# Attention scores from three fp32r products instead of one fp32 product, in a kernel of windowed attention and a gated convolution

## The chip, the cores and the metric

One core of a Trainium2 chip. The metric is the device time of one execution in microseconds. Before the change it was 666.89 us, the median of three runs (666.77 to 667.21).

The engines are called PE (TensorE's matmuls; PEld is its weight loads), DVE (VectorE), ACT (ScalarE), POOL (GpSimd) and SP (the queue that issues the DMAs).

## The reference

Eight batches, eight heads, 576 positions, heads of 64. Attention looks back over a window of 128 positions, with a bias that falls linearly with distance (a slope per head). Its output, 4608 tokens of 512 features, goes through a feed-forward part with a convolution over three neighbouring positions and a sigmoid gate. Everything is computed in fp32 accuracy.

```
scores = q @ k.T / sqrt(64) - slope[h] * |i - j|,  masked to 0 <= i - j < 128
attn   = softmax(scores);  x = attn @ v            # heads put side by side: (8, 576, 512)
h      = relu(x @ w_in)                            # 512 -> 1024
conv   = sum over k of conv_w[k] * h shifted by k-1, zero beyond a batch's ends
out    = (h * sigmoid(conv)) @ w_out               # 1024 -> 512
```

## The kernel before, in words

The 4608 tokens are 36 tiles of 128. A batch has 4.5 tiles, so tiles 0, 9, 18 and 27 begin a batch exactly, tiles 4, 13, 22 and 31 contain a boundary in their middle, and tiles 5, 14, 23 and 32 begin half a tile into a batch. A tile's queries see its own keys and those of the tile before; a batch's exact first tile needs only its own.

[...] The type fp32r holds a rounded fp32 number and is one instruction. The kernel writes a number as a high half (its fp32r rounding) and a low half (the rest), and takes three products: high by high, high by low, low by high. Before the change it did so for the up-projection (L424) and the down-projection (L501), while the scores (L287, L289), the product with the values (L377) and the transposes (L263, L347) were fp32.

Steps of a tile t, by the short names that the order uses; u is one of two groups of four heads:

- LD, LV: fetch q and k, and v (L255), by SP. Q: eight transposes of q and k on PE (L263) into two PSUM tiles. QO: ACT copies both to SBUF (L267), into one of three slots of `qkT_all` (t modulo 3).
- S: scores (L289, in exact first tiles L287). For each u there are two PSUM tiles, for the even and the odd heads; an even head lies in rows 0 to 63, an odd one in rows 64 to 127, and the two are issued in turn.
- MA: DVE merges the keys of the previous tile into the own ones under a mask (L305; at batch boundaries a second mask), then scales and adds the bias (L318). RM: row extreme (L322). X: exponentials on ACT (L327), two heads to a piece. N: DVE normalizes (L338 to L340). T: transposes on PE (L347). RL: ACT copies them out (L352). SEL: POOL cuts the window's two triangles (L358, L361).
- AV: product with the values on PE (L377). XH: ACT writes its high half into the ring `ring` (L388). XL: DVE writes the low half (L392). XF: every fourth tile, a small copy at the ring's end (L397).

Steps of the feed-forward part run over 18 chunks of 256 tokens, four steps s to a chunk, two blocks of 128 of the 1024 features to a step:

- UH: up-projection, 12 matmuls of 256 columns a block (L424). HH: relu on ACT (L437). Z: the middle tap on ACT (L443) into `zp`, of which there is one buffer, so that the next Z waits for the gate of the step before. CV: the outer taps on DVE (L456); a chunk with a batch boundary inside is cut, four pieces for two. TH: tanh on ACT (L464). GT: the gate on DVE (L469). GH: high half on ACT (L479). GL: low half on POOL (L484).
- D: down-projection, 12 matmuls of 512 columns (L501). OB: after a chunk's fourth step ACT copies the two sums out and SP stores them (L514, L516).

Weights come as 16 blocks and the taps as one small block, and they arrive as 64-bit floating-point numbers that the kernel turns into high and low halves itself: F fetch, CL and SG on POOL (L161, L171), RS on ACT (L166), SH and V on DVE (L175; L181 or L185, then L188), H the high half on ACT (L195), then P and W for the low half. For a block in LOW_POOL or LOW_DVE the low half is one subtraction on that engine (L214); otherwise PE forms it in PSUM with three instructions (L206, L207) and ACT copies it out (L216). A block in SIGNS has its sign prepared on POOL, and DVE then needs one operation (L181) where it otherwise needs two (L175, L185).

Five PSUM buffers with the tag `tr` are shared by transposes, scores, the product with the values, the up-projections and the weights' low halves. Each engine takes its instructions in the order in which the pieces stand in three written lists: OPENING (tiles 0 to 5, steps 0 to 5, all weights), PERIOD (once for each tile from 6 to 35, with two steps) and TAIL (what is left). A number in PERIOD is relative: S0 is this tile, Q1 the next, AV-1 the last.

Of the kernel before, what the change touches and what calls it, by code (L numbers as in the profile page):

```python
# [21 lines left out]
def tile_alibi_window_attention_conv_glu(  # L22
# [154 lines left out]
    def w_bits(b):  # L177
        st, g = wst.pop(b), wgs[b]
        lo, hi = st[..., 0], st[..., 1]
        if b in SIGNS:  # L180
            nc.vector.scalar_tensor_tensor(  # L181
# [40 lines left out]

    raws, vraw, pts, sms, es, pas, rls, avs = {}, {}, {}, {}, {}, {}, {}, {}
    ring = cpool.tile([P, 2, NCC, RING + 4], F32R, name="ring")
# [37 lines left out]
        pts[t, u] = ps  # L264

    def qkT_out(t, u):
        nc.scalar.copy(out=qkT_all[:, t % SLOTS, u], in_=pts.pop((t, u)))  # L267

    def window(t):
        first = (t * P) % S  # L270
        slot = t % SLOTS
        if slot:
            win, prev, cur = slice(slot - 1, slot + 1), 0, 1
        else:
            win, prev, cur = slice(0, SLOTS, SLOTS - 1), 1, 0
        return first, slot, win, prev, cur

    def scores(t, u):
        first, slot, win, prev, cur = window(t)

        pss = [pst.tile([P, NG, 2, P], F32, name=f"sc{t}_{u}_{a}", tag="tr") for a in range(2)]
        for g in range(NG):
            for a in range(2):
                rows = slice(a * D, (a + 1) * D)
                qt = qkT_all[rows, slot, u, 0, g, :]
                if first == 0:
                    nc.tensor.matmul(pss[a][:, g, cur], qt, qkT_all[rows, slot, u, 1, g, :], start=True, stop=True)  # L287
                else:
                    nc.tensor.matmul(pss[a][:, g], qt, qkT_all[rows, win, u, 1, g, :], start=True, stop=True)  # L289
        sms[t, u] = pss  # L290


    def merge(t, u, a):
# [8 lines left out]
        shp = [P, 2, P]

        def put(mask, data):
            nc.vector.copy_predicated(out=s_cur, mask=mask.unsqueeze(1).to_broadcast(shp), data=data)  # L305
# [12 lines left out]
        nc.vector.scalar_tensor_tensor(out=heads, in0=s_cur, scalar=-0.125, in1=b, op0=ALU.mult, op1=ALU.add)  # L318
# [208 lines left out]
    TILE = {
        "LD": load, "LV": loadv, "Q": qk, "QO": qk_out, "S": scores, "MA": merge, "RM": rowmax,  # L530
        "X": lambda t, u, h: exps(t, u, range(2 * h, 2 * h + 2)),
        "N": normal, "T": attnT, "RL": attn_out, "SEL": select, "AV": av, "XH": x_hi, "XL": x_lo, "XF": xfin,
    }
# [23 lines left out]
    OPENING = """
    LD0 F1 F3 F0 CL0 CL1 Q0 LD1 QO0 S0.0 RS0 RS1 S0.1 LV0 H4 MA0.1.1 SG0 F2 CL3 MA0.1.0 LD2 MA0.0.1 RM0.1
    MA0.0.0 Q1 F4 CL2 LV4 QO1 X0.1.1 V0 S1.0 F7 X0.1.0 MA1.0.1 SG1 RM0.0 MA1.0.0 S1.1 H0 MA1.1.1 F5 Q2 P0
    RS2 N0.1 LD3 LV1 QO2 LD4 V1 S2.0 T0.1 X0.0.1 X0.0.0 F8 H1 MA1.1.0 F13 N0.0 W0 P1 RM1.0 X1.0.0 F10 X1.0.1  # L560
    W1 MA2.0.1 SG2 Q3 F9 SH5 CL4 CL7 LV2 RS4 QO3 SH4 RS3 V2 N1.0 T0.0 RL0.0 CL5 H2 S2.1 T1.0 SG3 RM1.1 S3.0
    P2 MA2.1.0 RL0.1 X1.1.0 X1.1.1 MA2.1.1 Q4 LD5 RL1.0 V3 RM2.1 MA2.0.0 MA3.0.0 H3 RM2.0 F6 X2.1.1 W2
    X2.1.0 RS5 N1.1 SEL0.0 SEL0.1 AV0 LV3 X2.0.0 P3 XF1 V4 W3 X2.0.1 T1.1 LD6 QO4 RS7 SH8 SEL1.0 V5 P4 CL13
    CL8 S3.1 N2.0 SG7 MA3.0.1 T2.0 RL1.1 H5 N2.1 LD8 MA3.1.0 SEL1.1 AV1 MA3.1.1 T2.1 W4 XH0 P5 RS8 RM3.0
    RL2.0 XH1 RM3.1 X3.1.1 SEL2.0 RL2.1 CL10 V8 X3.1.0 F11 SH9 X3.0.1 F12 XL1 SEL2.1 F16 S4.0 CL6 AV2 CL9 W5
    RS6 XF0 SG6 H8 XL0 MA4.0.0 XH2 N3.1 Q5 V7 P8 X3.0.0 QO5 H7 W8 P7 N3.0 SH10 XL2 T3.1 W7 CL11 RS9 UH0.0
    RS11 UH0.1 RL3.1 LD7 V6 T3.0 MA4.0.1 H6 RS10 HH0.1 HH0.0 SG11 RL3.0 S4.1 RM4.0 V10 Z0.0 V9 CV0.0 Z0.1
    UH1.0 CV0.1 H10 HH1.0 TH0 V11 RS13 F15 H9 GT0 W6 XF2 LV5 W10 UH1.1 UH3.1 HH1.1 XF3 Z1.0 UH2.0 Z1.1 CL15
    MA4.1.1 CV1.1 CV1.0 GH0 MA4.1.0 SEL3.0 SEL3.1 UH2.1 TH1 X4.0.0 GT1 X4.0.1 UH3.0 HH3.0 RM4.1 N4.0 HH2.0
    P9 SH12 AV3 HH3.1 CL12 HH2.1 T4.0 X4.1.0 SG13 W9 V13 S5.1 X4.1.1 N4.1 RS12 T4.1 H13 Z2.1 XH3 GL0 F14  # L570
    S5.0 Z2.0 V12 RL4.0 MA5.1.0 RL4.1 SEL4.0 H11 SEL4.1 W13 H12 CV2.0 CV2.1 AV4 P11 CL16 MA5.0.1 D0 TH2 GH1
    Z3.1 GT2 Q6 XH4 MA5.1.1 CV3.1 XL4 Z3.0 W12 GH2 XL3 XF4 GL1 RS16 MA5.0.0 CL14 W11 CV3.0 RS15 UH4.1 RS14
    RM5.0 RM5.1 SG15 SG14 LV6 X5.1.1 X5.0.1 V15 V14 UH5.1 H15 UH5.0 UH4.0 D1 TH3 X5.0.0 GT3 SG16 N5.0 X5.1.0
    T5.0 V16 HH4 H14 QO6 H16 Z4.1 GL2 W14 RL5.0 GH3 W15 LV7 D2 N5.1 CV4.1 T5.1 HH5 GL3 Z4.0 SEL5.0 W16 CV4.0
    TH4 RL5.1 GT4 SEL5.1 Z5.1 GH4 GL4 CV5.1 Z5.0 CV5.0 TH5 D3 GT5 OB3
    """
# [50 lines left out]
```

## Time and profile before

| | us |
|---|---|
| median of three runs | 666.89 |
| the profiled execution's own time | 667.78 |
| its span in the trace | 665.5 |
| scores of tile 6 begin | 104.28 |
| scores of tile 35 begin | 602.87 |
| one plain period (tile 20) | 17.08 |

The profile shows one execution. [...] A row of a timeline has the start, the length, the engine, the line of the kernel, the operation, what it writes and reads, and how many instructions are merged in it; in square brackets stands idle time before it and who ended it. A row of a group has busy time and the mean length of one in ns behind the bar, then idle time before the group. A row of a stretch has for each engine the busy time, with the number of instructions in brackets, then the granted clock of PE as a share, the share of the DMA engines and GB/s.

### The profile page before, as it was taken

The page shows a single profiled execution, that of the slowest core. Times are in us where ns is not written, and L with a number is a line of the kernel's source. Part 1 is how long each engine was busy: PE and PEld are TensorE (multiplying, and loading weights), DVE is VectorE, ACT ScalarE, POOL GpSimd, SP SyncE. Part 2 cuts the span into 40 slices and gives each one's busy share as a digit, 9 for nine tenths or more (in the row PEclk, how much of TensorE's full clock was granted, in tenths as well). Part 3 has the DMA queues.
Part 4 walks back from the last instruction along what each step waited for, and adds up shares of the span by engine and source line. Part 5 has one row for each costly group of instructions (what it writes and reads, how often), then busy time and mean ns, then how long its engine had stood idle before and what let it go on. Part 6 is the DMA issues. An engine that isn't in the chain of part 4 may idle for free.

```text
span 665.5 us, 13256 instructions
## 1 busy us (share of the span) xinstructions
PE 634.5 (95%) x4860; PEld 547.8 (82%) x4860; DVE 516.4 (78%) x1177; ACT 434.3 (65%) x1202; POOL 214.3 (32%) x319
## 2 busy tenths in 40 slices
PE   4888799999999999999999999999999999999997
PEld 3467587887888788888888888988888888888995
DVE  5998997778777888787777788778778888788554
ACT  3876775665766676666666766666676656666553
POOL 2353544333233322233233222223222233333321
PEclk9989999999999999999999999999999999999999
DMA  9878003232323223131403140404040403000001
...
DMA packets 120099, 47.00 MB, mean 71 GB/s; under 512 B 113356, under 2 KB 113380, under 8 KB 120036
## 3 DMA queue, kind: packets, MB, share of 16 engines
...
q14 instruction: 25, 0.20, 0.1%
...
## 4 chain that ended last, share of the span: by engine, by line
PE 56%; DVE 28%; ACT 9%; issue 4%; DMA 1%; SPq 0%; POOL 0%; POOLq 0%; DVEq 0%; ACTq 0%
PE p L424 21%; PE o L501 19%; DVE zp L456 12%; PE sc L289 5%; PE av L377 5%; ACT zp L443 4%; DVE sc L305 3%; DVE z L469 3%; PE pa L347 3%; DVE e L318 3%; PE pt L263 3%; ACT e L327 2%; DMA rqk<-in_k_dram 1%; DVE ring L392 1%; ACT zp L464 1%
## 5 line engine op out<-in xcount | busy, mean ns | idle before, releaser
L424 PE MATMUL p<-ring,wi 128*128 128x256 f32 (+1 forms) x1728 | 221.3, 284 | 8.3 <-DVE ring L397 3.6
L424 PEld LDWEIGHTS p<-ring,wi 128*128 128x128 f32 x1728 | 211.9, 189 | 14.5 <-issue 4.2
L456 DVE SCALAR_TENSOR_TENSOR zp<-hh,cw,zp 128x256 f32<-128x256 f32 (+7 forms) x384 | 162.2, 422 | 76.0 <-ACT zp L443 65.3
L501 PE MATMUL o<-wo,gh 128*128 128x512 f32 x576 | 186.1, 404 | 0.6 <-ACT ob L514 0.6
L327 ACT ACTIVATE e<-e,st 128x128 f32<-128x128 f32 x288 | 112.4, 393 | 96.3 <-DVE st L322 96.3
L358 POOL TENSOR_SCALAR_AFFINE_SELECT rl<-rl 128x512 f32<-128x512 f32 x64 | 41.1, 642 | 280.9 <-ACT rl L352 280.9
L501 PEld LDWEIGHTS o<-wo,gh 128*128 128x128 f32 x576 | 103.1, 188 | 26.8 <-issue 5.2
L484 POOL TENSOR_TENSOR gl<-z,gh 128x512 fp32r<-128x512 f32 x71 | 91.2, 1284 | 86.7 <-ACT gh L479 74.6
L501 PE MATMUL o<-wo,gl 128*128 128x512 f32 x288 | 114.7, 398 | 0.4 <-POOL gl L484 0.2
L443 ACT ACTIVATE zp<-hh,cw 128x256 f32<-128x256 f32 x144 | 69.0, 479 | 24.0 <-DVE z L469 15.8
L469 DVE SCALAR_TENSOR_TENSOR z<-zp,hh 128x512 f32<-128x512 f32 (+1 forms) x73 | 49.8, 682 | 29.3 <-ACT zp L464 27.1
L464 ACT ACTIVATE zp<-zp 128x512 f32<-128x512 f32 (+1 forms) x73 | 42.3, 579 | 45.1 <-DVE zp L456 42.4
L289 PE MATMUL sc<-qkT_all 64*128 64x256 f32 x512 | 68.4, 396 | 1.9 <-ACT rl L352 1.3
L377 PEld LDWEIGHTS av<-rl,rv 128*64 128x64 f32 x1088 | 59.2, 138 | 12.4 <-issue 8.2
L377 PE MATMUL av<-rl,rv 128*64 128x128 f32 x1088 | 68.8, 278 | 0.3
L501 PEld LDWEIGHTS o<-wo,gl 128*128 128x128 f32 x288 | 54.1, 188 | 13.7 <-POOL gl L484 1.2
L318 DVE SCALAR_TENSOR_TENSOR e<-sc,bias 128x256 f32<-128x256 f32 x144 | 61.1, 424 | 5.0
L289 PEld LDWEIGHTS sc<-qkT_all 64*128 64x128 f32 x512 | 48.5, 189 | 14.3 <-issue 5.6
L361 POOL TENSOR_SCALAR_AFFINE_SELECT rl<-rl 128x512 f32<-128x512 f32 x72 | 46.6, 647 | 36.9 <-ACT rl L352 29.2
L305 DVE COPY_PREDICATED sc<-m_prev,sc 128x256 f32<-128x256 uint8 x128 | 53.7, 420 | 1.7 <-PE sc L289 1.7
L327 ACT ACTIVATION_READ_ACCUMULATOR e<-e,st 128x1 f32 x288 | 54.4, 189 | 0.0
L340 DVE TENSOR_TENSOR e<-e,st 128x512 f32<-128x512 f32 x72 | 50.4, 700 | 2.5
...
## 6 DMA issues: line engine op xcount, KB each, us to landing
...
```

The lines of the kernel that those rows point to most:

```text
L289: nc.tensor.matmul(pss[a][:, g], qt, qkT_all[rows, win, u, 1, g, :], start=True, stop=True)
L305: nc.vector.copy_predicated(out=s_cur, mask=mask.unsqueeze(1).to_broadcast(shp), data=data)
L318: nc.vector.scalar_tensor_tensor(out=heads, in0=s_cur, scalar=-0.125, in1=b, op0=ALU.mult, op1=ALU.add)
L327: nc.scalar.activation(out=e[:, j, :], in_=e[:, j, :], func=AF.Exp, bias=st[:, 0, j : j + 1], scale=-1.0, accum_out=st[:, 1, j : j + 1],)
L340: nc.vector.tensor_tensor(out=e, in0=e, in1=st[:, 2, :].unsqueeze(2).to_broadcast([P, HU, P]), op=ALU.mult)
L377: nc.tensor.matmul(ps[a * D : (a + 1) * D, u * NG + g], vraw[tt][:, u * HU + j], rl[:, side, j], start=n == 0, stop=n == len(sides) - 1,)
L424: nc.tensor.matmul(ps, a[:, cc, f * P : (f + 1) * P], ring[:, i, cc, cols], start=n == 0, stop=n == last)
L443: nc.scalar.activation(out=zps[s][:, ff, :], in_=hhs[s][:, ff, 1 : 1 + CW], func=AF.Copy, scale=cw[:, 1, f : f + 1])
L456: nc.vector.scalar_tensor_tensor(out=z[:, ff, a:cut], in0=hh[:, ff, a + kk : cut + kk], scalar=cw[:, kk, f : f + 1], in1=z[:, ff, a:cut], ...
L469: nc.vector.scalar_tensor_tensor(out=zgs[s][:, ff], in0=zps[s][:, ff], scalar=1.0, in1=hhs[s][:, ff, 1 : 1 + CW], op0=ALU.add, op1=ALU.mult,)
L484: nc.gpsimd.tensor_tensor(out=gl, in0=zgs.pop(s), in1=as32(gh), op=ALU.subtract)
L501: nc.tensor.matmul(oos[c][m], g[:, ff, ms], w[:, f, :], start=f == 0 and n == 0, stop=f == NFC - 1 and n == 2)
```

## The change

- From tile 9 on (`SPLIT = 9`), ACT's evacuation of the transposed queries and keys (QO) writes fp32r, which is the high half. A new step QL subtracts this on DVE from the PSUM tile and writes the low half to `qkT_low`. The scores become three fp32r products, each summed in PSUM. Tiles 0 to 8 keep the fp32 product. QL for tile t+1 stands in PERIOD of tile t.
- Transposed queries and keys have two slots in place of three. The fp32 tile and the fp32r tile share one buffer, which changes its type at tile 9.
- The PSUM tiles of the transposes are given back by QL from tile 9 on, by QO before.
- OPENING, PERIOD and TAIL are written anew.
- SIGNS grows by blocks 5, 8, 9, 10 and 12. LOW_POOL has one block (9) in place of four, LOW_DVE gets block 6 as well. Eleven blocks take PE's way to the low half instead of nine.

The core of the diff:

```
-    SIGNS = {0, 1, 2, 3, 6, 7, 11, 13, 14, 15, 16}
-    LOW_POOL = {6, 10, 12, 13}
-    LOW_DVE = {14, 15, 16}
+    SIGNS = {0, 1, 2, 3, 5, 6, 7, 8, 9, 10, 11, 12, 13, 14, 15, 16}
+    LOW_POOL = {9}
+    LOW_DVE = {6, 14, 15, 16}
...
-    SLOTS = 3
+    SLOTS = 2
+    SPLIT = 9
     NG = HU // 2
-    qkT_all = cpool.tile([P, SLOTS, 2, 2, NG, P], F32, name="qkT_all")
+    qkT_low = cpool.tile([P, SLOTS, 2, 2, NG, P], F32R, name="qkT_low")
+    qkTs = {}
+
+    def qkT_of(t):
+        kind = F32 if t < SPLIT else F32R
+        if kind not in qkTs:
+            qkTs[kind] = apool.tile([P, SLOTS, 2, 2, NG, P], kind, name=f"qkT{t}", tag="qkT", bufs=1)
+        return qkTs[kind]
...
     def qkT_out(t, u):
-        nc.scalar.copy(out=qkT_all[:, t % SLOTS, u], in_=pts.pop((t, u)))
+        nc.scalar.copy(out=qkT_of(t)[:, t % SLOTS, u], in_=pts.pop((t, u)) if t < SPLIT else pts[t, u])
+
+    def qkT_rest(t, u):
+        if t >= SPLIT:
+            nc.vector.tensor_tensor(
+                out=qkT_low[:, t % SLOTS, u], in0=pts.pop((t, u)), in1=as32(qkT_of(t)[:, t % SLOTS, u]), op=ALU.subtract
+            )
...
+        keys = win if first else slice(slot, slot + 1)
+        top = qkT_of(t)
+        passes = ((top, top),) if t < SPLIT else ((top, top), (top, qkT_low), (qkT_low, top))
         for g in range(NG):
...
+            for n, (tq, tk) in enumerate(passes):
+                for a in range(2):
+                    rows = slice(a * D, (a + 1) * D)
+                    to = pss[a][:, g] if first else pss[a][:, g, cur]
+                    of = tk[rows, keys, u, 1, g, :] if first else tk[rows, slot, u, 1, g, :]
+                    nc.tensor.matmul(
+                        to, tq[rows, slot, u, 0, g, :], of, start=n == 0, stop=n == len(passes) - 1
+                    )
```

PERIOD before:

```
S0.0 S0.1 AV-1 XH-1 MA0.1.0 MA0.0.0 XL-1 D-2 XF-1 MA0.0.1 UH0.1 GH-1 RM0.0 MA0.1.1 UH0.0 X0.0.1 X0.0.0
HH0 Z0.0 RM0.1 LD3 UH1.1 Z0.1 N0.0 Q1 UH1.0 CV0.0 X0.1.1 GL-1 LV2 QO1 CV0.1 X0.1.0 HH1 T0.0 D-1 TH0
RL0.0 N0.1 GT0 T0.1 Z1.1 Z1.0 SEL0.0 CV1.0 RL0.1 SEL0.1 GH0 OB-1 OB-2 GL0 CV1.1 TH1 GT1
```

PERIOD after:

```
S0.0 S0.1 AV-1 MA0.0.1 D-2 XH-1 LV2 XL-1 XF-1 MA0.0.0 RM0.0 X0.0.0 MA0.1.0 UH0.1 UH0.0 UH1.1 GH-1 X0.0.1
HH0 MA0.1.1 Z0.0 Z0.1 Q1 LD3 RM0.1 UH1.0 X0.1.0 GL-1 X0.1.1 N0.0 QO1 CV0.0 HH1 T0.0 D-1 CV0.1 N0.1 TH0
OB-2 RL0.0 Z1.1 GT0 SEL0.0 Z1.0 QL1 T0.1 RL0.1 SEL0.1 CV1.0 GH0 CV1.1 OB-1 TH1 GL0 GT1
```

OPENING before begins `LD0 F1 F3 F0 CL0 CL1 Q0 LD1 QO0 S0.0 RS0 RS1 S0.1 LV0`; after, it begins `LD0 Q0 F1 QO0 S0.0 CL1 RS1 S0.1 MA0.0.0 MA0.1.1 LD1 F2 SG1 Q1`. In TAIL the pieces are the same ones; D-1 stands later, behind the up-projections of the next steps.

More of the change, by code (lines that the diff above doesn't have):

```diff
@@ L271, in window @@
         slot = t % SLOTS
[L272 to L275, printed above, removed]
+        win, prev, cur = slice(0, SLOTS), 1 - slot, slot
         return first, slot, win, prev, cur
@@ L281, in scores @@
         pss = [pst.tile([P, NG, 2, P], F32, name=f"sc{t}_{u}_{a}", tag="tr") for a in range(2)]
+        keys = win if first else slice(slot, slot + 1)
+        top = qkT_of(t)
+        passes = ((top, top),) if t < SPLIT else ((top, top), (top, qkT_low), (qkT_low, top))
         for g in range(NG):
[L283 to L289, printed above, removed]
+            for n, (tq, tk) in enumerate(passes):
[6 more added lines that the diff above has]
+                    )
         sms[t, u] = pss
@@ L525, in qk_out, with qk_rest @@
             qkT_out(t, u)
+    def qk_rest(t):
+        for u in range(2):
+            qkT_rest(t, u)
     TILE = {
-        "LD": load, "LV": loadv, "Q": qk, "QO": qk_out, "S": scores, "MA": merge, "RM": rowmax,
+        "LD": load, "LV": loadv, "Q": qk, "QO": qk_out, "QL": qk_rest, "S": scores, "MA": merge, "RM": rowmax,
         "X": lambda t, u, h: exps(t, u, range(2 * h, 2 * h + 2)),
@@ L557, in tile_alibi_window_attention_conv_glu @@
     OPENING = """
[L558 to L572, printed above, removed]
@@ L573, in tile_alibi_window_attention_conv_glu @@
-    RM5.0 RM5.1 SG15 SG14 LV6 X5.1.1 X5.0.1 V15 V14 UH5.1 H15 UH5.0 UH4.0 D1 TH3 X5.0.0 GT3 SG16 N5.0 X5.1.0
-    T5.0 V16 HH4 H14 QO6 H16 Z4.1 GL2 W14 RL5.0 GH3 W15 LV7 D2 N5.1 CV4.1 T5.1 HH5 GL3 Z4.0 SEL5.0 W16 CV4.0
-    TH4 RL5.1 GT4 SEL5.1 Z5.1 GH4 GL4 CV5.1 Z5.0 CV5.0 TH5 D3 GT5 OB3
+    LD0 Q0 F1 QO0 S0.0 CL1 RS1 S0.1 MA0.0.0 MA0.1.1 LD1 F2 SG1 Q1 MA0.1.0 V1 QO1 S1.0 F0 MA0.0.1 MA1.0.1 LD2
+    CL2 CL0 RM0.0 S1.1 RS2 RS0 F7 H1 F3 X0.0.0 SG2 F5 X0.0.1 MA1.1.1 SG0 LV0 Q2 MA1.0.0 F4 P1 QO2 V0 F9
@@ new lines, in tile_alibi_window_attention_conv_glu @@
+    RM0.1 S2.1 F8 N0.0 LD3 W1 X0.1.1 V2 MA1.1.0 MA2.1.1 T0.0 X0.1.0 RL0.0 H0 SEL0.0 P0 RM1.1 H2 S2.0 W0 CL3
+    MA2.1.0 CL5 X1.1.1 CL4 RS3 P2 N0.1 RM2.1 RS5 LD4 F10 T0.1 MA2.0.1 LV3 W2 MA2.0.0 RL0.1 RM1.0 X1.1.0 F13
+    RM2.0 SH4 X2.1.0 N1.1 RS4 X2.0.1 LV2 X2.0.0 Q3 SG3 SG5 T1.1 QO3 H4 X2.1.1 V4 N2.0 T2.0 V5 CL7 S3.1 XF1
+    X1.0.0 SEL0.1 RL2.0 F6 S3.0 RL1.1 CL10 LV1 V3 X1.0.1 MA3.1.0 H5 P5 LD5 MA3.0.1 N1.0 Q4 H3 MA3.0.0 XF3
+    N2.1 CL8 F14 P3 T1.0 AV0 W5 RS7 SG7 V7 QO4 MA3.1.1 S4.0 MA4.0.1 RL1.0 RM3.0 W3 S4.1 F12 LD6 CL6 H7
@@ new lines, in tile_alibi_window_attention_conv_glu @@
+    SEL1.0 MA4.0.0 P7 P4 RS8 X3.0.1 F11 W7 XH0 T2.1 SEL1.1 RS10 X3.0.0 LV4 MA4.1.0 AV1 RL2.1 W4 SEL2.0 SG8
+    SEL2.1 V8 AV2 H8 XL0 RS6 RM4.0 XH1 Q5 N3.0 SG6 XH2 QO5 CL12 XF0 P8 CL9 CL13 V6 X4.0.1 XL1 XL2 W8 MA4.1.1
+    T3.0 H6 RM3.1 UH0.0 XF2 SG10 RM4.1 RS9 SG9 UH0.1 V10 HH0.0 X4.0.0 UH1.1 S5.1 F15 Z0.0 F16 H10 HH0.1
+    X4.1.1 W6 N4.0 RL3.0 RS13 UH2.0 V9 CV0.0 X4.1.0 X3.1.0 Z0.1 UH1.0 MA5.1.1 H9 CV0.1 SG13 CL14 V13 HH1.1
+    SEL3.0 P10 LV5 N4.1 CL16 HH2.0 X3.1.1 UH2.1 TH0 W9 W10 GT0 H13 P13 HH1.0 HH2.1 T4.0 RS12 RL4.0 MA5.1.0
@@ new lines, in tile_alibi_window_attention_conv_glu @@
+    Z1.0 GH0 Z1.1 W13 SG12 UH3.0 T4.1 RL4.1 CL11 RS11 N3.1 S5.0 CV1.1 MA5.0.0 LV6 CV1.0 UH3.1 T3.1 TH1 V12
+    RL3.1 H12 GT1 SEL4.0 SEL4.1 SEL3.1 HH3.1 Z2.1 AV4 RS16 GL0 CL15 P12 Z2.0 MA5.0.1 RM5.1 SG11 XH4 AV3 D0
+    X5.1.0 CV2.0 XL4 HH3.0 CV2.1 SG16 XH3 V11 W12 X5.1.1 GH1 XF4 Q6 TH2 H11 QO6 LD8 RS15 GT2 P11 XL3 N5.1
+    GL1 RM5.0 UH5.1 SG15 W11 Z3.1 X5.0.0 V16 UH5.0 RS14 UH4.1 CV3.1 T5.1 SG14 HH5 V15 Z3.0 UH4.0 V14 H16
+    X5.0.1 GH2 RL5.1 H15 H14 CV3.0 LD7 GL2 TH3 HH4 D1 N5.0 GT3 Z4.1 W14 W15 CV4.1 D2 W16 GH3 GL3 T5.0 D3
@@ L576, in tile_alibi_window_attention_conv_glu @@
+    Z4.0 RL5.0 SEL5.1 CV4.0 LV7 TH4 GT4 Z5.1 CV5.1 OB3 Z5.0 SEL5.0 CV5.0 GH4 TH5 GL4 GT5
     """
     PERIOD = """
-    S0.0 S0.1 AV-1 XH-1 MA0.1.0 MA0.0.0 XL-1 D-2 XF-1 MA0.0.1 UH0.1 GH-1 RM0.0 MA0.1.1 UH0.0 X0.0.1 X0.0.0
-    HH0 Z0.0 RM0.1 LD3 UH1.1 Z0.1 N0.0 Q1 UH1.0 CV0.0 X0.1.1 GL-1 LV2 QO1 CV0.1 X0.1.0 HH1 T0.0 D-1 TH0
-    RL0.0 N0.1 GT0 T0.1 Z1.1 Z1.0 SEL0.0 CV1.0 RL0.1 SEL0.1 GH0 OB-1 OB-2 GL0 CV1.1 TH1 GT1
+    S0.0 S0.1 AV-1 MA0.0.1 D-2 XH-1 LV2 XL-1 XF-1 MA0.0.0 RM0.0 X0.0.0 MA0.1.0 UH0.1 UH0.0 UH1.1 GH-1 X0.0.1
@@ L582, in tile_alibi_window_attention_conv_glu @@
+    HH0 MA0.1.1 Z0.0 Z0.1 Q1 LD3 RM0.1 UH1.0 X0.1.0 GL-1 X0.1.1 N0.0 QO1 CV0.0 HH1 T0.0 D-1 CV0.1 N0.1 TH0
+    OB-2 RL0.0 Z1.1 GT0 SEL0.0 Z1.0 QL1 T0.1 RL0.1 SEL0.1 CV1.0 GH0 CV1.1 OB-1 TH1 GL0 GT1
     """
     TAIL = """
-    OB2 UH0.1 UH0.0 AV-1 GH-1 HH0 Z0.0 XH-1 CV0.0 Z0.1 UH1.0 XF-1 CV0.1 XL-1 TH0 UH1.1 D-2 OB4 UH2.1 HH1
-    GL-1 UH2.0 HH2 GT0 UH3.1 UH4.1 UH3.0 Z1.0 CV1.0 GH0 GL0 Z1.1 CV1.1 TH1 UH4.0 Z2.1 Z2.0 D-1 GT1 OB-2
-    CV2.0 CV2.1 TH2 HH3 UH5.0 GH1 Z3.1 Z3.0 D0 GT2 GL1 CV3.0 HH4 GH2 CV3.1 D1 TH3 GT3 Z4.0 Z4.1 GL2 GH3
@@ L588, in tile_alibi_window_attention_conv_glu @@
-    CV4.0 GL3 UH5.1 CV4.1 HH5.0 OB1 TH4 HH5.1 GT4 Z5.0 Z5.1 OB-1 D2 CV5.0 TH5.0 GT5.0 GH4 GH5.0 GL5.0 CV5.1
-    TH5.1 OB3 GT5.1 GL4 D3 OB0 GH5.1 GL5.1 D4 D5 OB5
+    UH0.1 GH-1 XF-1 UH0.0 AV-1 HH0 D-2 Z0.0 XH-1 CV0.0 UH1.0 Z0.1 OB-2 XL-1 OB-1 CV0.1 UH1.1 UH3.1 TH0 UH2.1
+    UH2.0 GT0 HH1 Z1.0 GL-1 CV1.0 GH0 OB0 Z1.1 HH2 CV1.1 UH3.0 UH5.0 TH1 UH4.1 GT1 HH3 Z2.1 GH1 Z2.0 CV2.0
+    UH4.0 CV2.1 TH2 GT2 Z3.1 OB2 D-1 GL0 Z3.0 CV3.0 CV3.1 TH3 OB3 GL1 D0 GH2 HH4 GT3 Z4.0 D1 Z4.1 CV4.0 OB1
+    CV4.1 UH5.1 TH4 HH5.0 GL2 Z5.0 GT4 HH5.1 GH3 Z5.1 GH4 CV5.0 GL3 TH5.0 GT5.0 CV5.1 TH5.1 GT5.1 GL4 D2 D3
@@ L590, in tile_alibi_window_attention_conv_glu @@
+    GH5.0 GH5.1 OB4 GL5.0 GL5.1 D4 D5 OB5
     """
```

## Prediction

> **What bounds the kernel now.** I read the page first, for the engines' shares and the chain.
>
> ```profile
> span 665.5 us, 13256 instructions
> PE 634.5 (95%) x4860; PEld 547.8 (82%) x4860; DVE 516.4 (78%) x1177; ACT 434.3 (65%) x1202; POOL 214.3 (32%) x319
> PE 56%; DVE 28%; ACT 9%; issue 4%; DMA 1%; SPq 0%; POOL 0%; POOLq 0%; DVEq 0%; ACTq 0%
> ```
>
> A share over the whole span mixes stages, so the busy times of three stretches came next: the opening (to the scores of tile 6), the thirty periods with the scores of tiles 6 to 35, and the tail.
>
> ```profile
> 0.00:104.28 104.28, 84.04 (x565) 62.39 (x565) 89.59 (x199) 71.45 (x200) 46.77 (x70) 0.98 0.58 147
> 104.28:602.87 498.59, 492.14 (x3897) 434.47 (x3896) 392.23 (x907) 331.41 (x930) 150.55 (x226) 1.00 0.25 60
> 602.87:665.50 62.63, 58.38 (x401) 50.98 (x400) 34.59 (x72) 31.43 (x73) 17.02 (x25) 1.00 0.07 26
> ```
>
> The columns after the length are PE, weight loads, DVE, ACT and POOL. DVE leads in the opening (89.59 of 104.28); afterwards PE does. PE's timeline over one plain period (tile 20) shows how tightly:
>
> ```profile
> 345.44 2.00 PE L289 MATMUL sc<-qkT_all 64*128 64x256 f32 x16
> 347.37 1.97 PE L377 MATMUL av<-rl,rv 128*64 128x128 f32 x32
> ...
> 352.17 4.45 PE L424 MATMUL p<-ring,wi 128*128 128x256 f32 x36
> 356.45 1.03 PE L263 MATMUL pt<-ident_r,rqk 128*128 128x128 f32 x8
> 357.24 1.68 PE L424 MATMUL p<-ring,wi 128*128 128x256 f32 x12
> 358.76 0.60 PE L347 MATMUL pa<-ident_r,e 128*128 128x128 f32 x4
> 359.11 0.71 PE L501 MATMUL o<-wo,gh 128*128 128x512 f32 x2
> ...
> 362.52 0.70 PE L289 MATMUL sc<-qkT_all 64*128 64x256 f32 x4
> ```
>
> No row names a releaser, and each starts where the one before lets go: 17.08 us from scores to scores is PE work alone. Time taken out of PE there comes off the period, if nothing else becomes late. What made PE wait in the thirty periods:
>
> ```profile
> PE p L424 <- DVE ring L397: 3.6, 3, 1.6
> PE p L424 <- DVE ring L392: 2.0, 2, 1.2
> ```
>
> Both are the up-projection waiting for the attention output's low half or the copy behind it on DVE, 5.6 us in five periods, after periods in which DVE had more to do.
>
> **The scores.** Before, a tile's eight products of fp32 are 16 matmuls in 8 pairs (two heads, rows 0 to 63 and 64 to 127). After, 24 in 12 pairs. Two narrow looks at one burst, one pair apart, and the burst of a batch's first tile:
>
> ```profile
> 329.23 0.70 PE L289 MATMUL sc<-qkT_all 64*128 64x256 f32 x4
> 329.23 0.92 PE L289 MATMUL sc<-qkT_all 64*128 64x256 f32 x6
> 312.82 1.16 PE L287 MATMUL sc<-qkT_all 64*128 64x128 f32 x16
> 313.91 2.15 PE L377 MATMUL av<-rl,rv 128*64 128x128 f32 x32
> ```
>
> A pair costs 0.92 - 0.70 = 0.22 us, so 8 x 0.22 = 1.76 of the 1.93 us from 345.44 to 347.37, and 0.17 for entering and leaving. The nearest row for an fp32r matmul of 256 columns is L424: 36 from 352.17 to 356.45, 4.28/36 = 0.119 us each. No fp32r matmul of 64 rows is in this trace. If two of them on different rows run side by side as the fp32 ones do, a pair costs 0.119 and a tile 12 x 0.119 + 0.17 = 1.60 us, 0.33 less. If they don't, 24 x 0.119 + 0.17 = 3.03, 1.10 more. I take the first: the fp32 pairs are nearest in form, and only the operands' type changes. Weight loads could prevent it, since 12 pairs in 1.43 us want two loads every 0.119. L287 shows 16 loads of that shape in 313.91 - 312.82 = 1.09 us, 0.068 each, so two in 0.136 at worst, with matmuls that may themselves set that pace; a pair of 0.136 would save 0.13 a tile instead of 0.33.
>
> [...]
>
> Of tiles 9 to 35, 24 have 256 columns: 24 x -0.33 = **-7.9 us**. Tiles 9, 18 and 27 have 128: now 8 x 0.136, then 12 x between 0.06 (half of 0.119) and 0.136, that is -0.4 to +0.5 each; I take 0.
>
> **The low halves.** Two subtractions a tile on DVE, from PSUM into fp32r, 512 columns: the form of L392. The conversions on DVE matter too, since batch boundaries cut them.
>
> ```profile
> L392 DVE TENSOR_TENSOR ring<-av,ring 128x512 fp32r<-128x512 f32 x36 | 24.3, 680 | 0.0
> L456 DVE SCALAR_TENSOR_TENSOR zp<-hh,cw,zp 128x192 f32<-128x192 f32 x32 | 13.5, 422 | 7.8 <-ACT zp L443 7.0
> L456 DVE SCALAR_TENSOR_TENSOR zp<-hh,cw,zp 128x63 f32<-128x63 f32 x32 | 9.2, 289 | 1.1
> 348.83 0.42 DVE L305 COPY_PREDICATED sc<-m_prev,sc 128x256 f32<-128x256 uint8 x1
> 356.94 2.06 DVE L456 SCALAR_TENSOR_TENSOR zp<-hh,cw,zp 128x256 f32<-128x256 f32 x4 [1.50 <-ACT zp L443]
> 360.51 0.69 DVE L469 SCALAR_TENSOR_TENSOR z<-zp,hh 128x512 f32<-128x512 f32 x1
> 362.26 2.06 DVE L456 SCALAR_TENSOR_TENSOR zp<-hh,cw,zp 128x256 f32<-128x256 f32 x4 [1.06 <-ACT zp L443]
> 365.05 0.69 DVE L469 SCALAR_TENSOR_TENSOR z<-zp,hh 128x512 f32<-128x512 f32 x1 [0.72 <-ACT zp L464]
> ```
>
> Each costs 0.68, 1.36 us a period, 27 x 1.36 = 37 us in all. The new order puts them behind the first gate (360.51) and ahead of the second conv (362.26), exactly where DVE idles 1.06 us for ACT's scaling. So DVE's round grows by 0.30 only. Behind them on DVE are the second conv, its gate and the next tile's masks; the next scores wait for them, as do the PSUM buffers that they read, now held until then.
>
> Are they in time? ACT leads up to them:
>
> ```profile
> 355.29 0.60 ACT L437 ACTIVATE hh<-p 128x512 f32<-128x512 f32 x1 [0.98 <-PE p L424]
> 355.92 0.99 ACT L443 ACTIVATE zp<-hh,cw 128x256 f32<-128x256 f32 x2
> 357.62 1.04 ACT L267 COPY qkT_all<-pt 128x512 f32<-128x512 f32 x2
> 359.34 0.58 ACT L437 ACTIVATE hh<-p 128x512 f32<-128x512 f32 x1
> 359.82 0.59 ACT L464 ACTIVATE zp<-zp 128x512 f32<-128x512 f32 x1
> ```
>
> In the new order ACT does relu, scalings, four exponentials, the evacuation, relu, tanh without a break. From scores to the first relu is 355.29 - 345.44 = 9.85, less 0.33: 9.5. Relu and scalings 1.6, exponentials 1.6 (357.62 less 355.92 + 0.99 covers two, about 0.8), evacuation 1.05, relu and tanh 1.1: tanh ends at 14.9. Gate 0.7, first subtraction at 16.3, second at 17.0. The new period is 17.08 - 0.33 = 16.75. The first half of the scores needs the first subtraction, 0.4 us to spare; the second half starts 0.8 after the first and needs the second, 0.5 to spare. So in a plain period the cost is nothing, covered by PE's own 16.75; without that cover it would be 0.7 for each subtraction.
>
> Heavy periods differ. DVE's busy time (third column behind the length) in this plain period:
>
> ```profile
> 345.44:362.52 17.08, 17.08 (x137) 15.15 (x137) 12.32 (x28) 11.85 (x33) 5.33 (x8) 1.00 0.45 108
> ```
>
> Of its 4.76 idle, 1.50, 1.06 and 0.72 stand in the rows above; of the other 1.48 I count half as gaps between instructions that no order removes. So the work takes 12.32 + 0.7 = 13.0; plus 1.36, plus the 0.72 that the second gate always waits, 15.1 of 16.75. A cut conv has two pieces for each one (0.42 + 0.29 and a gap, against 2.06/4 = 0.51): 0.23 more, 1.8 in a period with two convs cut, which is twelve periods, ten of them from tile 9 on. Masks at a batch boundary add four copies of 0.42 or more, about 2.0, in six periods. Such a round is about 17.0, 0.3 over PE's 16.75; sixteen of them come to 5 us if nothing absorbs it. Before, by the same count, the round was 13.0 + 1.06 + 0.72 + 1.9 = 16.7 against 17.08, and yet 5.6 us of waits appeared, 0.35 a heavy round: the count is short by some 0.7. With that the new round is 17.7, and the upper bound 16 x 0.95 - 5.6 = +9.6. Two things absorb it: a plain round gives 1.6 back, and the attention output's low half now stands behind one tile's mask pair instead of two (0.42 from 348.83 and a like scaling, some 0.8 us), which is what those waits hung on. So between -5 (the old waits gone, no new ones) and +9.6; I take **+0.5**, near the row that these waits have now, with new waits for scores in place of old ones for the up-projection.
>
> **Moves at no cost.** Two slots: the evacuation of tile t+1 overwrites tile t-1, whose keys the scores of t read in the first 1.6 us of the period; the evacuation comes at 12.7. The shared buffer at tile 9 waits for tile 8's scores, equally long done. Casting to fp32r on ACT instead of copying: the same instruction but for the type it writes, inside a chain with 0.4 us to spare. The hi cast of the gate moves behind the first exponentials; its low half is then ready on POOL near 10, and the down-projection that reads it starts at 13.3. LV2 and LD3 change place on the SP queue; their buffers were free a period earlier.
>
> **Opening and tail.** Rows of the opening, DVE's and PE's:
>
> ```profile
> DVE sc L305 <- PE sc L287: 4.0, 1, 4.0
> DVE sc L305 <- PE sc L289: 1.7, 2, 1.5
> L175 DVE TENSOR_SCALAR wst<-wst 128x512 uint32<-128x512 uint32 x5 | 2.5, 508 | 0.0
> L185 DVE SCALAR_TENSOR_TENSOR wst<-wst 128x512 uint32<-128x512 uint32 x5 | 3.4, 681 | 0.0
> L181 DVE SCALAR_TENSOR_TENSOR wst<-wst 128x512 uint32<-128x512 uint32 x11 | 10.0, 913 | 0.7 <-POOL wst L171 0.7
> L206 PE MATMUL pw<-wg,ident_r 128*128 128x512 f32 x18 | 9.9, 630 | 4.0 <-DVE e L318 3.5 <-ACT qkT_all L267 0.4
> ```
>
> Five blocks go from shift and merge (0.508 + 0.681) to one operation (0.913): -1.4 us of DVE; one more low half on DVE is like L392's, +0.7 to +0.8. Two blocks more take the PE route, 9.9/9 = 1.1 us each and a third matmul, +2.2 to +3.8 of PE, which had 20 us free here. Tile 1 is now fetched after one weight block instead of three, so the wait of 1.7 goes; the 4.0 for tile 0 stays. POOL gets five more signs and three fewer subtractions, at 46.77 busy of 104.28: nothing. Sum: -0.6 - 1.7 + part of PE's, **-1.0**, between -4 (a third of DVE's idle 14.7) and +4 (PE's all on the path). The tail does the same work, PE-bound (58.38 of 62.63), its last four down-projections covering the last gate: 0, within 1.
>
> **Sum.** -7.9 + 0 + 0.5 - 1.0 = -8.4. Against the profiled execution's 667.78 (2.3 over its span) 659.4; against the median 666.89 **658.5 us**.
>
> **The rivals.** *A: the fp32r halves don't run side by side.* +1.10 x 24 = +26.4, +1.0 for the three short tiles; the period becomes 18.2, over DVE's heavy round, so the 5.6 us of waits vanish; opening -1.0. 666.9 + 20.8 = 687.7. For it: no such matmul is in the trace. Against: fp32 pairs do so here, and 16 narrow loads came in 1.09 us. It decides as soon as a pair costs over 1.76/12 = 0.147 us. [...] Chance 0.14. *B: DVE becomes the bound.* The sixteen heavy rounds pass their overhang on undiminished, +9.6 less the 0.8 that the low half's new place is worth: -7.9 + 8.8 - 1.0, 666.8 us, no change. For it: the waits already there. Against: 1.6 us of slack in each plain round. Chance 0.12. *C: the scores' gain is there and the opening loses 4 while B happens half:* 666.9 - 7.9 + 4.4 + 4 = 667.4; chance 0.06.
>
> **Numbers.** My case 0.68. Its own range: the scores between -10 and -6 (a pair's 0.22 is known to 0.01 or so), waits and opening as above but not all at one end at once: 652 to 665. B and C lie about 667 and, with the opening's other end, reach 670. The range 652 to 670 leaves out A. A difference under 0.2% (1.3 us) can't be told from none. Faster 0.72 (my case and B's better side), same 0.08, slower 0.20 (A and B's worse side).
>
> **What would show it.** Right: scores bursts of 1.6 us with 24 matmuls; plain periods of 16.75; DVE's 1.06 us before the second conv gone, with 0.68 us subtractions in it; waits of the up-projection for the ring smaller, some waits of scores for the low halves in heavy periods; S1 earlier in the opening. Wrong: bursts near 3 us, or plain periods in which the scores wait for the subtraction.

## The result and the profile after

The changed kernel takes 650.95 us (median of four runs, 650.04 to 651.56); the kernel before took 667.05 beside it. The ratio is 0.9757, with a 95% interval from 0.974 to 0.9774. The forecast was 658.5, in a range from 652 to 670: the direction was right, the gain twice as large, and the time just below the range.

The page of the changed kernel, in the lines that answer to those shown of the kernel before:

```profile
span 649.8 us, 13737 instructions
PE 628.3 (97%) x5082; PEld 551.2 (85%) x5082; DVE 548.7 (84%) x1227; ACT 434.8 (67%) x1204; POOL 211.3 (33%) x321
PE 83%; DVE 13%; issue 2%; DMA 1%; ACT 1%; POOL 0%; SPq 0%; DVEq 0%; ACTq 0%; POOLq 0%
```

DVE is busy 32 us longer, about the time of the new subtractions, and yet its part of the chain that ended last fell from 28% to 13%. The three stretches (to the scores of tile 6, on to those of tile 35, the tail):

```profile
0.00:101.00 101.00, 84.83 (x571) 63.70 (x571) 88.50 (x195) 73.16 (x203) 45.08 (x73) 0.95 0.59 152
101.00:587.96 486.96, 485.67 (x4106) 436.61 (x4106) 425.52 (x960) 330.09 (x930) 149.36 (x225) 1.00 0.27 62
587.96:649.80 61.84, 57.83 (x409) 50.94 (x408) 34.66 (x73) 31.51 (x73) 16.85 (x25) 1.00 0.07 26
```

Opening -3.3 us, thirty periods -11.6, tail -0.8: -15.7 in the two profiled executions. PE's and DVE's timelines of one plain period:

```profile
336.46 0.38 PE L303 MATMUL sc<-qkT 64*128 64x256 f32 x2
336.69 0.28 PE L303 MATMUL sc<-qkT_low,qkT 64*128 64x256 f32 x2
336.81 0.28 PE L303 MATMUL sc<-qkT,qkT_low 64*128 64x256 f32 x2
...
338.09 1.97 PE L393 MATMUL av<-rl,rv 128*64 128x128 f32 x32
...
353.22 0.38 PE L303 MATMUL sc<-qkT 64*128 64x256 f32 x2
```

```profile
351.22 0.69 DVE L485 SCALAR_TENSOR_TENSOR z<-zp,hh 128x512 f32<-128x512 f32 x1 [0.50 <-ACT zp L480]
351.83 1.28 DVE L280 TENSOR_TENSOR qkT_low<-pt,qkT 128x512 fp32r<-128x512 f32 x2
353.02 2.05 DVE L472 SCALAR_TENSOR_TENSOR zp<-hh,cw,zp 128x256 f32<-128x256 f32 x4
355.80 0.69 DVE L485 SCALAR_TENSOR_TENSOR z<-zp,hh 128x512 f32<-128x512 f32 x1 [0.72 <-ACT zp L480]
```

Pairs start 0.12 us apart (336.69 to 336.81) while their rows are 0.28 long, so rows overlap. The burst, from start to start, is 1.63 us (336.46 to 338.09), the period 353.22 - 336.46 = 16.76; forecast were 1.60 and 16.75. The subtractions fill the place where DVE idled 1.06 us; the conv behind them has no idle time in brackets any more. What made PE wait in the thirty periods is one line. Before, there were 5.6 us in two lines for the ring, and 0.6 us for copying out the sums of the down-projection:

```profile
PE p L440 <- DVE ring L413: 1.1, 3, 0.8
```

### The profile page after: what moved, and what is told of

The parts are those of the page before. It is cut to its first block, busy times and chain, and to the rows that moved or that the text cites. A ratio compares the mean times of both kernels' runs of the same rounds, so it can differ in the third digit from the quotient of the medians.

```text
span 649.8 us, 13737 instructions
## 1 busy us (share of the span) xinstructions
PE 628.3 (97%) x5082; PEld 551.2 (85%) x5082; DVE 548.7 (84%) x1227; ACT 434.8 (67%) x1204; POOL 211.3 (33%) x321
## 4 chain that ended last, share of the span: by engine, by line
PE 83%; DVE 13%; issue 2%; DMA 1%; ACT 1%; POOL 0%; SPq 0%; DVEq 0%; ACTq 0%; POOLq 0%
PE p L440 30%; PE o L517 29%; PE av L393 8%; PE sc L303 8%; PE pt L272 4%; PE pa L363 4%; DVE zp L472 2%; DVE sc L321 2%; DVE wg L188 1%; DVE e L334 1%; DVE wst L181 1%; DVE st L338 1%; DVE ring L408 1%; DVE e L356 1%; DVE z L485 1%
## 5 line engine op out<-in xcount | busy, mean ns | idle before, releaser
L393 PE MATMUL av<-rl,rv 128*64 128x128 f32 x1088 | 67.2, 276 | 1.2 <-PE pa L363 0.7
L303 PE MATMUL sc<-qkT 64*128 64x256 f32 (+1 forms) x360 | 55.2, 357 | 1.4 <-DVE e L334 1.2
L338 DVE TENSOR_REDUCE st<-e 128x4 f32<-128x512 f32 x72 | 49.2, 685 | 2.1
```

Source lines behind the costliest of these rows:

```text
L303: nc.tensor.matmul(to, tq[rows, slot, u, 0, g, :], of, start=n == 0, stop=n == len(passes) - 1)
L393: nc.tensor.matmul(ps[a * D : (a + 1) * D, u * NG + g], vraw[tt][:, u * HU + j], rl[:, side, j], start=n == 0, stop=n == len(sides) - 1,)
```

## The experiments

The missing 7 us had to come from the waits and the opening. Two theories: the *order theory* says that the new lists, with the weights' sets, took the old waits and shortened the opening, whatever type the scores have; the *scores theory* says that the shorter bursts and the low halves did it. In the first four experiments one part is made at a time.

**All orders, fp32 scores.**

```
-    SPLIT = 9
+    SPLIT = 99
```

> The changed kernel with fp32 scores in all tiles (no low halves, no fp32r products); all orders, two slots and the weights' sets as changed. Order theory (the new orders alone took the up-projection's waits and shortened the opening): plain periods of 17.08, waits of PE for the ring at most 1 us, scores of tile 6 at about 101, in all about 658 us, 7 to 8 more than the changed kernel and 8 to 9 less than the kernel before. Scores theory (the shorter scores and the low halves brought all of it): 664 to 667 us.

655.92 us, ratio to the kernel before 0.9836 (0.9807 to 0.9865). More than two thirds of the gain is there without a single low half of queries or keys; the order theory holds. The scores then add 5.0 us (655.92 to 650.95).

**The new PERIOD alone**, in the kernel before:

```
-    PERIOD = """ (before)
+    PERIOD = """ (after, without QL1)
```

> The kernel before with the new PERIOD alone (without its subtractions), fp32 scores, three slots. Order theory: PE's waits for the ring fall from 5.6 us to under 1.5, the stretch from the scores of tile 6 to those of tile 35 falls by 4 to 5.5 us, in all about 662 us. Scores theory: no change, 667 us.

662.29 us, ratio 0.9927 (0.9898 to 0.9956). PE's waits in the thirty periods:

```profile
PE o L501 <- ACT ob L514: 0.6, 1, 0.6
PE p L424 <- DVE ring L397: 0.3, 1, 0.3
```

The 5.6 us for the ring became 0.3, with PE's work unchanged.

**The new OPENING and weight sets alone**, in the kernel before:

```
-    SIGNS, LOW_POOL, LOW_DVE, OPENING (before)
+    SIGNS, LOW_POOL, LOW_DVE, OPENING (after)
```

> The kernel before with the new OPENING and the new sets for the weights alone. Order theory: the scores of tile 6 begin 3 us earlier, near 101, and the time is 663.5 to 664. If instead the opening's 3 us need something of the rest of the change (two slots, the new PERIOD behind it): no change, 667 us.

662.66 us, ratio 0.9933 (0.9908 to 0.9958); the scores of tile 6 begin at 100.65. It needs nothing of the rest. PERIOD alone and the opening alone take 4.8 and 4.4 us off the median beside them (667.10), together 9.2 of the 11.2 us of all orders; what the rest belongs to was not separated.

**The split scores in the old lists:**

```
     (old lists and sets, PERIOD:)
-    RL0.0 N0.1 GT0 T0.1 Z1.1
+    RL0.0 N0.1 GT0 QL1 T0.1 Z1.1
```

With two slots the old OPENING overwrites some keys too early: in tiles 2, 3 and 4 the second group of heads sees the keys of a later tile in place of the one before. The amount of work is unchanged.

> The split scores with the old OPENING, PERIOD and TAIL and the old sets; the subtractions stand between the first gate and the second conv; two slots, since three don't fit beside the low halves, so the opening may be longer. To be read from the stretch of tiles 6 to 35 (498.6 before, 487.0 changed). Order theory: plain periods of 16.76, but the ring's waits stay at 5.6 us or grow (to 8 or more by the term of the prediction), stretch 491 to 495. Scores theory: waits gone as in the changed kernel, stretch near 487.

664.99 us, ratio 0.9968 (0.9946 to 0.999). The stretch of thirty periods and the waits in it:

```profile
105.45:602.96 497.51, 489.15 (x4105) 438.05 (x4104) 420.19 (x960) 331.06 (x929) 150.32 (x225) 1.00 0.26 60
```

```profile
PE p L440 <- DVE ring L413: 4.4, 3, 2.1
PE p L440 <- DVE ring L408: 2.9, 3, 1.5
```

Plain periods are 16.76 here too, but the stretch is only 1.1 us shorter than before (498.59). The profiled execution is the longest of ten (667.67), so the stretch lies at the long end. 7.7 us came out of the scores, and 6.6 were given back, more than either theory expected: 1.2 by the tiles of 128 columns (below), the rest by waits. Those for the ring grew to 7.3 us, and behind the longest, 2.15 us, 17 matmuls of the up-projection took 3.61 us, where 36 took 4.49 behind a wait of 1.62 us in the kernel before; the next run shows the granted clock behind such a wait, and its price. So the old order gives back about as much as rival B feared. But it does so through the ring's waits, not through long rounds of DVE as such: the period of tile 12, in which two convs are cut, is 16.76 here too.

**What in PERIOD took the waits?** One edit in the changed kernel puts the low half of the attention output behind two mask pairs again:

```
-    XL-1 XF-1 MA0.0.0 RM0.0
+    MA0.0.0 XL-1 XF-1 RM0.0
```

> The changed kernel with one edit in PERIOD: the low half of the attention output (XL, XF) stands behind two mask pairs again instead of one. If its place took the waits away: plain periods stay at 16.76, PE's waits for the ring go from 1.1 us back to 5 or more, 654 to 656 us. If the waits went for another reason (the order on ACT, say): 651 us.

657.98 us, ratio 0.9846 (0.9821 to 0.9871): 7 us are gone. PE's waits in the thirty periods, then the timeline's row of the longest, then two stretches behind it with the granted clock (third value from the end):

```profile
PE p L440 <- DVE ring L413: 3.9, 3, 1.9
PE p L440 <- DVE ring L408: 2.2, 2, 1.5
```

```profile
227.72 2.67 PE L440 MATMUL p<-ring,wi 128*128 128x256 f32 x14 [1.95 <-DVE ring L413]
```

```profile
229.60:231.50 1.90, 1.90 (x11) 1.90 (x11) 1.80 (x5) 0.76 (x4) 1.41 (x2) 0.50 0.00 0
233.40:236.00 2.60, 2.60 (x25) 2.60 (x24) 1.81 (x4) 2.57 (x12) 0.00 (x0) 1.00 0.00 0
```

The ring's waits are back at 6.1 us. After the wait of 1.95 us the granted clock was 0.50 from 229.60 to 231.50: the row counts 11 matmuls in 1.90 us, and a row of the same length at a clock of 1.00 in the same work counts 18 (the changed kernel, 343.20 to 345.10). The stretches around it have mean clocks of 0.72 (227.72 to 229.60) and 0.88 (231.50 to 233.40); from these I estimate the half clock at 228.55 to 231.96, about 3.4 us. That period took 20.48 us, 3.7 over a plain one, for 1.95 of waiting; in the changed kernel it takes 17.74.

The same move the other way, alone in the kernel before:

```
-    MA0.1.0 MA0.0.0 XL-1 D-2 XF-1
+    MA0.1.0 XL-1 D-2 XF-1 MA0.0.0
```

> The kernel before with one edit in PERIOD: XL and XF stand behind one mask pair instead of two. If the place alone took the waits: PE's waits for the ring fall from 5.6 us to 1 or 2, stretch of tiles 6 to 35 near 494.5, 662 to 663.5 us, as the new PERIOD did. If the other moves are needed: over 665 us.

664.36 us, ratio 0.996 (0.9938 to 0.9981). The ring's waits did fall:

```profile
PE p L424 <- DVE ring L397: 1.5, 3, 0.7
PE o L501 <- ACT ob L514: 0.6, 1, 0.6
PE pa L347 <- DVE e L340: 0.5, 2, 0.4
```

From 5.6 to 1.7 (0.2 for L392 stands further down), but new small ones appear (the transposes wait for the normalization), and the gain, 2.6 us, is about half of PERIOD's and lies between the two expectations. So the place is what most of these waits hung on, and PERIOD's other moves are needed for the rest; they were not tried one by one.

Further on the same way, ahead of all masks:

```
-    AV-1 MA0.0.1 D-2 XH-1 LV2 XL-1 XF-1 MA0.0.0
+    AV-1 D-2 XH-1 LV2 XL-1 XF-1 MA0.0.1 MA0.0.0
```

> The changed kernel with the low half of the attention output (XL, XF) ahead of all masks of the next tile. If its place behind DVE's other work sets the up-projection's remaining waits: the ring's 1.1 us go, and about as much of the time, 650 us. Against it: DVE then idles until ACT's high half is there, some 0.5 us a period, which heavy periods pass on: 651 to 655 us.

650.6 us, ratio 0.9764 (0.9743 to 0.9785): level. The ring's waits are gone, and transposes now wait 0.9 us for exponentials on ACT.

**Where the subtractions stand:**

```
-    GT0 SEL0.0 Z1.0 QL1 T0.1 RL0.1 SEL0.1 CV1.0 GH0 CV1.1 OB-1
+    GT0 SEL0.0 Z1.0 T0.1 RL0.1 SEL0.1 CV1.0 GH0 CV1.1 QL1 OB-1
```

> The changed kernel with the two subtractions behind the second conv instead of in DVE's idle time ahead of it. If the next scores have nothing to spare beyond half a microsecond, as the prediction's walk has it: they wait about 2 us in each of 27 periods, near 700 us. If the low halves are hidden anywhere: 651 us.

775.15 us, ratio 1.1621 (1.158 to 1.1663), 124 us over the changed kernel, more than twice what was expected. PE's timeline of one burst, then the same burst as a stretch, with the granted clock:

```profile
488.03 0.38 PE L303 MATMUL sc<-qkT 64*128 64x256 f32 x2
490.49 0.58 PE L303 MATMUL sc<-qkT_low,qkT 64*128 64x256 f32 x2 [2.08 <-DVE qkT_low L280]
...
492.79 0.41 PE L303 MATMUL sc<-qkT,qkT_low 64*128 64x256 f32 x2
```

```profile
490.49:493.13 2.64, 2.64 (x22) 2.42 (x22) 1.99 (x4) 0.00 (x0) 1.01 (x2) 0.50 0.00 0
```

The wait of 2.08 us is what the walk said; what it lacked is the granted clock of 0.50 after it: 0.21 us from pair to pair instead of 0.12. The gain thus depends on the subtractions standing ahead of the second conv.

**Do the row halves run side by side?** First the three products of one head in a row:

```
-            for n, (tq, tk) in enumerate(passes):
-                for a in range(2):
+            for a in range(2):
+                for n, (tq, tk) in enumerate(passes):
```

> The changed kernel with the three products of one head issued in a row and then those of the other, so that neighbours in the queue share their rows. If the gain hangs on two row halves side by side: bursts of 2.7 to 3.1 us instead of 1.6, 24 x 1.1 to 1.4 us less the 2 us of waits that go, 672 to 678 us. If the fp32r products are cheap whatever their neighbours: 651 us.

651.12 us, ratio 0.9754 (0.9738 to 0.9771): no change, against the first expectation. But the trace still shows pairs:

```profile
335.39 0.39 PE L303 MATMUL sc<-qkT 64*128 64x256 f32 x2
335.61 0.29 PE L303 MATMUL sc<-qkT_low,qkT 64*128 64x256 f32 x2
335.73 0.29 PE L303 MATMUL sc<-qkT,qkT_low 64*128 64x256 f32 x2
```

In the queue three even ones (one of each form) stand ahead of three odd ones; two of each form run together, so the odd head's first (335.39) overtook the even head's second (335.61) and third (335.73). So the edit had not taken the pairing away, and the halves were put further apart:

```
-        for g ...: for n ...: for a in range(2): matmul    # S0.0: group 0, S0.1: group 1
+        # S0.0: a = 0 of both groups (12 matmuls); S0.1: a = 1 of both groups
+        for u in range(2): for g ...: for n ...: matmul
```

> The changed kernel with, from tile 9 on, all 12 matmuls of the even heads (rows 0 to 63, both groups) ahead of all 12 of the odd heads (rows 64 to 127). When the halves stood three apart in the queue, they still ran side by side. If PE runs ahead in its queue for the other rows at any such distance: bursts of 1.6 us, about 651 us. If it doesn't reach 12 ahead: the bursts take 24 x 0.119 us or near it, 2.7 to 3.1 us, and the time is 670 to 680 us.

675.67 us, ratio 1.0141 (1.0122 to 1.0159), 25 us more than the changed kernel:

```profile
344.50 0.38 PE L303 MATMUL sc<-qkT 64*128 64x256 f32 x1
344.73 0.28 PE L303 MATMUL sc<-qkT_low,qkT 64*128 64x256 f32 x1
...
345.56 0.28 PE L303 MATMUL sc<-qkT,qkT_low 64*128 64x256 f32 x1
345.56 0.39 PE L303 MATMUL sc<-qkT 64*128 64x256 f32 x2
345.79 0.29 PE L303 MATMUL sc<-qkT_low,qkT 64*128 64x256 f32 x2
345.91 0.29 PE L303 MATMUL sc<-qkT,qkT_low 64*128 64x256 f32 x2
346.02 0.28 PE L303 MATMUL sc<-qkT 64*128 64x256 f32 x1
...
347.18 0.33 PE L413 MATMUL av<-rl,rv 128*64 128x128 f32 x2
```

Nine run alone, three pairs where the two twelves meet, nine alone: the burst is 2.68 us, 1.05 more than in the changed kernel, and the period 17.81. The first odd matmul, thirteenth in the queue, starts with the ninth, four places ahead. So the gain hangs on the pairing. Rival A had its price right: it put 24 single steps at 3.03 us, and the 21 steps here come to 21 x 0.119 + 0.17 = 2.67.

**The opening.** Tile 1's queries and keys earlier, in the kernel before:

```
-    LD0 F1 F3 F0 CL0 CL1 Q0 LD1 QO0
+    LD0 F1 LD1 F3 F0 CL0 CL1 Q0 QO0
```

> The kernel before with one edit in OPENING: q and k of tile 1 are fetched after one weight block instead of three. If the late second tile is what the opening lost: DVE's wait of 1.7 us for its scores goes, the scores of tile 6 begin 1.5 to 3 us earlier, 664 to 665.5 us. If the weights that come later then hold DVE up by as much: 667 us.

669.84 us, ratio 1.0036 (1.0017 to 1.0054): slower, so this move alone does not bring what the new opening brings. The wait for the second tile fell by 0.6 us, and DVE waited 2.5 us for a weight block that came later. Then the old weight sets in the changed kernel, and two low halves moved from PE to POOL:

```
     (old_sets)
-    SIGNS, LOW_POOL, LOW_DVE (after); SG5 SG8 SG9 SG10 SG12, W9
+    SIGNS, LOW_POOL, LOW_DVE (before); SH5 SH8 SH9 SH10 SH12, P9 W9
     (pool_lows)
-    LOW_POOL = {9}
+    LOW_POOL = {9, 10, 13}
```

> The changed kernel with the old sets for the weights (five blocks back to two operations on DVE, low halves on POOL for blocks 6, 10, 12 and 13, nine blocks over PE) in the new OPENING. If DVE's work sets the opening: 1 us or a little more slower, scores of tile 6 near 102. If PE's two added blocks are on the path, as the prediction counted in part: 1 us faster or more.

> The changed kernel with the low halves of weight blocks 10 and 13 on POOL instead of PE and ACT. If PE's work for them is on the opening's path: 1 to 3 us faster. If DVE sets it: the same, 651 us, or slower where POOL's longer subtraction holds something up.

653.96 us (ratio 0.9817, 0.9798 to 0.9836) and 650.81 us (ratio 0.977, 0.9736 to 0.9805). The stretches of the opening in ld1_early, old_sets and pool_lows, in this order; DVE's busy time is the third behind the length:

```profile
0.00:107.03 107.03, 85.73 (x564) 64.01 (x565) 90.36 (x199) 71.23 (x200) 47.15 (x69) 0.94 0.58 143
```

```profile
0.00:102.89 102.89, 82.45 (x565) 63.27 (x565) 90.62 (x199) 72.28 (x201) 47.86 (x71) 0.95 0.58 149
```

```profile
0.00:97.99 97.99, 81.61 (x564) 63.12 (x564) 86.76 (x196) 73.02 (x202) 47.39 (x75) 0.97 0.63 157
```

Length less DVE's work, which is its idle time, is 12.3 for old_sets, 11.2 for pool_lows and 12.5 for the changed kernel (101.00 - 88.50), all with the new OPENING; with the old one it is 14.7 (104.28 - 89.59), and 16.7 when tile 1 is fetched early. One execution of each is not enough to divide the 3.3 us, though. With the new opening and sets the scores of tile 6 begin between 98.64 and 101.72 in eight profiled executions (the changed kernel, opening_only, orders_only, xl_back, xl_first, ql_late, by_head, halves_apart), on average at 100.2, with 87.5 us of DVE's work. With the old ones they begin between 102.42 and 105.45 in three (before, period_only, xl_early), on average at 104.1, with 89.6. So of 3.8 us about 2.1 are DVE's work and 1.7 its idle time. With the old sets in the new order they begin at 102.89, 2.7 later than the average with the new sets, near the 3 us that the old sets cost in the medians. So the sets seem to have brought the larger part, by one execution and one median. For pool_lows the profile's 3 us don't show in the median, and the interval is too wide to tell a gain from none.

The two variants that came out level, together:

```
     (xl_first's PERIOD)
-    LOW_POOL = {9}
+    LOW_POOL = {9, 10, 13}
```

> The changed kernel with the low half of the attention output ahead of all masks and the low halves of weight blocks 10 and 13 on POOL. If the opening's length follows DVE's work and neither variant touches it: level with the changed kernel, 650 to 651.5 us. If POOL's part shortens the opening by the 3 us that one profile showed: 647 to 648.5 us.

651.13 us, ratio 0.9774 (0.9745 to 0.9804): level with the changed kernel; in the profiled execution the scores of tile 6 begin at 101.18, so the 3 us of pool_lows did not come again. No version tried is faster than the changed kernel beyond the noise.

## Why the prediction was wrong, point by point

| term | forecast | measured |
|---|---|---|
| scores, 24 tiles of 256 columns | -7.9 | 24 x (16.76 - 17.08) = -7.7 |
| scores, tiles 9, 18, 27 | 0 | 3 x 0.40 (tile 18) = +1.2 |
| waits in the thirty periods | +0.5 | -11.6 + 7.7 - 1.2 = -5.1 |
| opening | -1.0 | -3.3 |
| tail | 0 | -0.8 |
| sum | -8.4 | -15.7 |

The direction was forecast right, but for the sake of the scores, and they brought 6.5 of the 15.7 us; most came from terms that the forecast put near nothing. The measured value for the waits is what is left of the stretch, not a sum of rows.

**The scores: right.** Pairs at 0.12 us, 0.32 off the period, the low halves in DVE's gap. All three conditions were tried: without most of the pairs +25 us, with the low halves behind that gap +124, without the new lists most of the gain is given back.

**The waits: this step failed.** "I take **+0.5**, near the row that these waits have now, with new waits for scores in place of old ones for the up-projection." The heavy rounds were read as too long for the period, since 5.6 us of waits had appeared although the count gave 16.7 against 17.08; from that the count was called 0.7 short. It was not the length of the round but one deadline in it: the low half of the attention output stood behind two mask pairs, and the up-projection wanted it. Three heavy periods of the changed kernel show it, one with one cut conv, one with two, and one with a cut conv and the masks of a batch boundary:

```profile
185.14:201.90 16.76, 16.76 (x146) 15.16 (x146) 14.20 (x33) 10.92 (x31) 5.23 (x8) 1.00 0.23 48
201.90:218.66 16.76, 16.76 (x146) 15.16 (x146) 15.13 (x38) 11.53 (x34) 5.06 (x9) 1.00 0.32 80
218.66:236.40 17.74, 16.98 (x145) 15.06 (x144) 16.08 (x38) 10.64 (x31) 5.08 (x9) 1.00 0.20 45
```

DVE is busy 15.13 of 16.76 us and the period is no longer than a plain one; only the third, at 16.08, stretches by 1.0, and 0.8 of that is again the wait for the ring. The prediction saw the move of the low half and gave it 0.8 us and a bound of -5, and the outcome, -5.1, lay at that bound. That the place decides is shown by xl_back, where it alone brings the ring's waits from 1.1 back to 6.1 us, and, in the kernel before, in part by xl_early. The range was wrong with it: its low end held the waits' and the opening's good ends not to come together, and they did.

**The opening: mis-sized, and for a reason that fell.** DVE is the busiest engine there, as read from the shares. But the wait for tile 1's scores, which the sum let go with -1.7, did not go. DVE's waits for scores in the changed opening, and its row for the weights' one operation:

```profile
DVE sc L321 <- PE sc L303: 6.5, 4, 3.8
L181 DVE SCALAR_TENSOR_TENSOR wst<-wst 128x512 uint32<-128x512 uint32 x16 | 11.4, 713 | 0.0
```

These waits are 6.5 us, where before they were 4.0 + 1.7 = 5.7. The work on the weights was mis-sized instead: the sum took -1.4 for five blocks at 0.913 us. The rows of L175, L185 and L181 were 2.5 + 3.4 + 10.0 = 15.9 us before and are 11.4 now, -4.5: five shifts and merges are gone, and an operation of L181 takes 0.713 on average, not 0.913. In other executions with the old sets the three rows come to between 14.6 (old_sets) and 15.5 (ld1_early); why L181 took longer in them stays open. PE's two added blocks, of which the sum counted part, show no cost in the medians (pool_lows, first_and_pool). DVE's waits for weights on ACT and POOL, 1.9 and 0.7 us before, are not in the changed opening; which move took them stays open.

**The first tiles: the bound's upper part.** The burst of tile 18:

```profile
303.93 0.33 PE L303 MATMUL sc<-qkT 64*128 64x128 f32 x2
...
305.10 0.28 PE L303 MATMUL sc<-qkT_low,qkT 64*128 64x128 f32 x2
305.21 0.28 PE L303 MATMUL sc<-qkT,qkT_low 64*128 64x128 f32 x2
305.42 0.77 PE L393 MATMUL av<-rl,rv 128*64 128x128 f32 x10
```

0.11 us from pair to pair with 128 columns, hardly less than 0.12 with 256, so here three products cost more than one fp32 product: 305.42 - 303.93 = 1.49 us against 1.09.

**The rivals.** A's mechanism is real, but its condition didn't hold; B and C didn't come. The tail's -0.8 was not looked into; executions with the same new tail differ by as much (61.8 us in xl_first, 62.9 in halves_apart).
